# h of the second layer by one level of Strassen's algorithm over pairs of token blocks, with weights read back from DRAM

## The chip, the cores and the metric

The kernel runs on one core of one Trainium2 chip. The metric is the device time in microseconds of one execution; the number for the kernel before is the median of 3 runs. The trace comes from one further profiled execution of the same program.

## The reference

Attention through packed queries feeds two feed-forward layers. Only the second layer is touched by the change: x has 4608 rows (tokens) of 512, `w_in` is 512 x 2048, `w_out` is 2048 x 512.

```python
def _moe2_ref(x, w_in, w_out):
    h = x @ w_in
    g = h * np.cos(h)
    return (g @ w_out).astype(np.float32)
```

Everything is in float32. The kernel multiplies in a rounded 32-bit format (F32R) and wins accuracy back by splitting each operand into a high and a low part: a product is then three products, high x high, low x high and high x low.

## The kernel before, in words

The last half of the span is the second layer. Its tokens are cut into nine blocks of 512 (t = 0 to 8), its 2048 features into 16 blocks of 128, taken two at a time in eight steps (s = 0 to 7). In a step, `h2` makes h for two feature blocks: per feature block three part products (`wa, ya`) times four slices k of the contraction, so 24 matmuls of 128 x 512 a step. `el_cos` then computes g = h cos h on ScalarE (ACT) and VectorE (DVE) in turns: round (L586), fraction (L589), sine (L595), square (L596), product with h (L599), high part `gh` (L605), low part `gl` (L608). `ymm2` multiplies g by the rows of `w_out`, 24 matmuls a step, into four banks of PSUM that collect over the eight steps; after the last step they are copied out and stored. TensorE (PE) runs `h2` of step s+1 between `h2` and `ymm2` of step s, so that `el_cos` has the time of 24 other matmuls and more.

The weights of the second layer stay in SBUF as 32 tiles of the pool `wp` (16 `w2in`, 16 `w2out`, each with a high and a low part), and fill that pool. They are converted from 64-bit inputs by `Conv` in the last two blocks of the first layer and in block t = 0. The layer's input y1 lies in DRAM; `loady` and `splity` bring and split the next block's slices during a block, with the subtraction on GpSimd (POOL). The order on every engine is the order of the code (a manual schedule). All DMAs are issued by SyncE's queue (SP), in order: a DMA that waits holds up those behind it.

Of the kernel before, what the change touches and what calls it, by code (L numbers as in the profile page):

```python
# [10 lines left out]
F32 = mybir.dt.float32  # L11
F32R = mybir.dt.float32r
# [31 lines left out]
PACK1, PACK = 3, 7  # L44
G0, G1, G = (0, 14, 12), (7, 8, 22, 25), (9, 11, 13, 15)
YLOAD, Y2LOAD, Y2SPLIT = 2, 118, 125
SGN = -2147483648


@with_exitstack  # L50
def fused_kernel(ctx, tc, qT, kT, v, pT, w1i, w1o, w2i, w2o, ident, out):
# [17 lines left out]
    psh = ctx.enter_context(tc.tile_pool(name="psh", bufs=2, space=PSUM))  # L69
# [17 lines left out]
    class Conv:  # L87
# [525 lines left out]
    def ymm2(t, s, st):  # L613
        conv2.need(w2out, 2 * s + 1)
        if s == 0:
            yps[t] = [psy.tile([128, DM], F32, tag="y", name="y") for _ in range(4)]
        tail = (t, s) == (NB2 - 1, NSTEP - 1)
        for part, m in (
            [(i, m) for m in range(4) for i in range(2)] if tail
            else [(i, m) for i in range(2) for m in range(4)]  # L620
        ):
            for x in range(2):
                f = 2 * s + x
                for wh, gg in (((0, "gh"), (1, "gh")) if part == 0 else ((0, "gl"),)):
                    nc.tensor.matmul(  # L625
                        out=yps[t][m], lhsT=st[gg][:, x, 128 * m:128 * m + 128],
                        rhs=w2out[f][:, wh, :],
                        start=(s == 0 and x == 0 and part == 0 and wh == 0),
                        stop=(s == NSTEP - 1 and x == 1 and part == 1),
                    )  # L630
        if s == NSTEP - 1:
            for m in range(4):
                if m < 2:
                    o = p2.tile([128, DM], F32, tag="o", bufs=2, name="o")
                else:
                    o = p2r.tile([128, DM], F32, tag="wt", bufs=2, name="o")
                if m % 2 == 0:
                    nc.scalar.activation(out=o, in_=yps[t][m], func=AF.Copy, scale=-TWO_PI)
                else:
                    nc.vector.tensor_scalar(  # L640
                        out=o, in0=yps[t][m], scalar1=-TWO_PI, scalar2=None, op0=ALU.mult
                    )
                r0 = t * TB + 128 * m
                nc.sync.dma_start(out=out[r0:r0 + 128, :], in_=o)
            del yps[t]
# [147 lines left out]
    for n, (blk, s) in enumerate(steps):  # L793
        if n == NSTEP * (NB - 2):
            open_p2r()
            p2r, conv2 = p2x["r"], p2x["conv"]
        if n == STEP_ORDERED:
            sched.__exit__(None, None, None)
            sched = tc.manual_schedule()
            sched.__enter__()  # L800
        st = {}
        h1(blk, s, st)
        el1(st)
        cv = conv2 if blk >= NB - 2 else conv
        cv.c_all()
# [115 lines left out]
```

## Time and profile before

| | us |
|---|---|
| median of 3 runs (lowest, highest) | 1599.37 (1599.35, 1600.77) |
| the profiled execution, its own time | 1600.74 |
| its span, first to last instruction | 1599.0 |
| first matmul of h in the second layer starts at | 801.7 |
| last matmul of the second layer starts at, in the span | 1594.7 |
| busy over the span: PE, DVE, ACT, POOL | 1523.6, 1011.8, 871.4, 218.1 |

Read it as a chain: 1.7 us lie around the span, the first layer takes about half of it and the second layer the other half. An engine's busy time says little by itself; what counts is which engine the others wait for in a stretch.

### The profile page before, as it was taken

How to read it: one execution, taken by the hardware profiler on the slowest of the kernel's cores; microseconds unless marked ns; L12 is line 12 of the kernel's file. 1: busy time of each engine (PE TensorE's matmuls, PEld its weight loads, DVE VectorE, ACT ScalarE, POOL GpSimd, SP SyncE). 2: the span in 40 equal slices, each digit the busy share in tenths (PEclk: the TensorE clock that was granted, in tenths of full speed). 3: DMA queues.
4: the chain of work that ended last, by engine and by line, in shares of the span. 5: the costliest groups of instructions: out<-in, count | busy, mean ns of one | idle time of the engine just before them, and what ended most of it. 6: DMA issues, size and time to landing. Idle time of an engine off the chain costs nothing.

```text
span 1599.0 us, 25218 instructions
## 1 busy us (share of the span) xinstructions
PE 1523.6 (95%) x10336; PEld 1321.6 (83%) x10336; DVE 1011.8 (63%) x1357; ACT 871.4 (54%) x1331; POOL 218.1 (14%) x154
## 2 busy tenths in 40 slices
PE   3789999999999999997898999999999999999999
PEld 1678888999999999997877788888888888888887
DVE  6999888787878788789979433333333333333333
ACT  4768665665666566676666444444444443444443
POOL 3633110100101010111224010100001010101000
PEclk6799999999999999999999999999999999999999
DMA  9423222211211121022334101001010101010000
GB/s 347 147 100 119 78 79 90 64 46 34 76 36 58 60 64 60 31 80 95 94 114 139 40 14 40 14 1 53 0 47 7 42 12 40 14 40 14 23 4 27
DMA packets 49138, 97.63 MB, mean 61 GB/s; under 512 B 4928, under 2 KB 26432, under 8 KB 49024
## 3 DMA queue, kind: packets, MB, share of 16 engines
q1 hardware_dynamic: 49024, 96.03, 18.2%
q8 instruction: 81, 1.33, 0.4%
q14 instruction: 33, 0.27, 0.1%
HBM read 74.78 MB, written 21.23 MB: 60 GB/s over the span
## 4 chain that ended last, share of the span: by engine, by line
PE 78%; DVE 13%; issue 4%; ACT 2%; DMA 2%; SPq 0%; POOL 0%; DVEq 0%; ACTq 0%; POOLq 0%
PE y L625 22%; PE h L564 22%; PE y L500 20%; PE h L438 10%; DVE wt L133 2%; DVE y L468 2%; DVE wt L143 2%; PE gp L400 2%; DVE wt L138 2%; DVE d L466 1%; DVE t L465 1%; DVE y L472 1%; DVE gl L485 1%; ACT wt L121 1%; PE sc L250 1%
## 5 line engine op out<-in xcount | busy, mean ns | idle before, releaser
L564 PE MATMUL h<-yhl,w2i 128*128 128x512 f32 x1728 | 403.2, 389 | 0.0
L564 PEld LDWEIGHTS h<-yhl,w2i 128*128 128x128 f32 x1728 | 324.4, 188 | 67.1
L500 PE MATMUL y<-gh,w1o 128*128 128x288 f32 x2048 | 311.3, 304 | 16.8 <-ACT gh L480 11.8
L500 PEld LDWEIGHTS y<-gh,w1o 128*128 128x128 f32 x2048 | 284.1, 191 | 45.9 <-ACT t L453 14.9
L625 PE MATMUL y<-w2o,gh 128*128 128x512 f32 x1152 | 274.6, 390 | 7.4 <-ACT gh L605 7.4
L625 PEld LDWEIGHTS y<-w2o,gh 128*128 128x128 f32 x1152 | 215.7, 188 | 55.2 <-ACT gh L605 10.9
L589 DVE SCALAR_TENSOR_TENSOR a<-a,h 128x1024 f32<-128x1024 f32 (+1 forms) x74 | 88.0, 1192 | 244.9 <-ACT a L586 244.9
L438 PE MATMUL h<-a,g 128*128 128x288 f32 x1536 | 230.5, 300 | 12.8 <-ACT w1i L121 6.6
L438 PEld LDWEIGHTS h<-a,g 128*128 128x128 f32 x1536 | 214.9, 192 | 17.0 <-ACT w1i L121 7.5
L586 ACT ACTIVATE a<-h 128x1024 f32<-128x1024 f32 (+1 forms) x74 | 74.1, 1005 | 243.1 <-PE h L564 241.6
L453 ACT ACTIVATE t<-h 128x576 f32<-128x576 f32 x128 | 83.2, 650 | 207.6 <-PE h L438 207.3
L599 DVE SCALAR_TENSOR_TENSOR a<-a,h 128x1024 f32<-128x1024 f32 (+1 forms) x74 | 88.1, 1192 | 143.3 <-ACT a L596 143.3
L500 PE MATMUL y<-gl,w1o 128*128 128x288 f32 x1024 | 160.0, 299 | 1.2 <-DVE gl L485 1.2
L500 PEld LDWEIGHTS y<-gl,w1o 128*128 128x128 f32 x1024 | 145.0, 191 | 1.5 <-DVE gl L485 1.4
L625 PE MATMUL y<-w2o,gl 128*128 128x512 f32 x576 | 142.8, 390 | 0.0
L553 POOL TENSOR_TENSOR yhl<-yr,yhl 128x512 fp32r<-128x512 f32 x34 | 60.1, 1768 | 549.6 <-ACT yhl L552 549.6
L608 DVE TENSOR_TENSOR gl<-a,gh 128x1024 fp32r<-128x1024 f32 (+1 forms) x74 | 88.4, 1196 | 73.3 <-ACT gh L605 73.2
L465 DVE TENSOR_TENSOR t<-h,t 128x576 f32<-128x576 f32 x128 | 95.3, 744 | 52.8 <-ACT u L454 52.5
L625 PEld LDWEIGHTS y<-w2o,gl 128*128 128x128 f32 x576 | 108.2, 188 | 22.5 <-DVE gl L608 0.2
L472 DVE COPY_PREDICATED y<-k,t 128x576 f32<-128x576 int16 x128 | 118.4, 925 | 11.6
L595 ACT ACTIVATE a<-a 128x1024 f32<-128x1024 f32 (+1 forms) x74 | 76.7, 1037 | 83.3 <-DVE a L589 83.3
L605 ACT ACTIVATE gh<-a 128x1024 fp32r<-128x1024 f32 (+1 forms) x74 | 76.6, 1036 | 83.1 <-DVE a L599 83.1
(79 smaller groups left out, 1541.8 us busy)
## 6 DMA issues: line engine op xcount, KB each, us to landing
y<-ye SPq DMA_DIRECT2D x80, 144.0 KB, 1.9
yr<-y SPq DMA_DIRECT2D x36, 256.0 KB, 3.5
out<-o SPq DMA_DIRECT2D x36, 256.0 KB, 2.1
st<-w1i SPq DMA_DIRECT2D x16, 512.0 KB, 7.4
v<-vv SPq DMA_DIRECT2D x16, 512.0 KB, 4.5
st<-w1o SPq DMA_DIRECT2D x16, 512.0 KB, 6.5
st<-w2i SPq DMA_DIRECT2D x16, 512.0 KB, 3.6
st<-w2o SPq DMA_DIRECT2D x16, 512.0 KB, 3.6
```

The lines of the kernel that those rows point to most:

```text
L438: nc.tensor.matmul(out=h[:, x, 0:HB], lhsT=gw[b, f // 4, half][:, ga, c0:c0 + 128], rhs=a2[b, half][:, aa, HB * j:HB * j + HB], start=(n = ...
L453: nc.scalar.activation(out=st["t"], in_=h, func=AF.Tanh)
L465: lambda: nc.vector.tensor_tensor(out=t, in0=hs, in1=t, op=ALU.subtract),
L472: lambda: nc.vector.copy_predicated(out=y, mask=k.bitcast(I16), data=t),
L500: nc.tensor.matmul(out=yps[blk][d][:, 0:HB], lhsT=w1out[f][:, wh, 128 * d:128 * d + 128], rhs=st[gg][:, x, :], start=(s in first and x == ...
L564: nc.tensor.matmul(out=h[:, x, :], lhsT=w2in[f][:, wa, 128 * k:128 * k + 128], rhs=yt[k][:, ya, :], start=(n == 0), stop=(n == 11),)
L589: nc.vector.scalar_tensor_tensor(out=a[:, x], in0=a[:, x], scalar=MAGIC, in1=h[:, x], op0=ALU.subtract, op1=ALU.subtract,)
L595: nc.scalar.activation(out=a[:, x], in_=a[:, x], func=AF.Sin, scale=PI)
L599: nc.vector.scalar_tensor_tensor(out=a[:, x], in0=a[:, x], scalar=1.0, in1=h[:, x], op0=ALU.subtract, op1=ALU.mult,)
L605: nc.scalar.activation(out=gh[:, x], in_=a[:, x], func=AF.Copy)
L608: nc.vector.tensor_tensor(out=gl[:, x], in0=a[:, x], in1=f32(gh[:, x]), op=ALU.subtract)
L625: nc.tensor.matmul(out=yps[t][m], lhsT=st[gg][:, x, 128 * m:128 * m + 128], rhs=w2out[f][:, wh, :], start=(s == 0 and x == 0 and part == 0 ...
```

## The change: what it does

Blocks t = 0 to 2 are computed as before (`NCL` = 3). The other six are taken as three pairs (t, t+1). For a pair and a pair of feature blocks F, let A be the four 128 x 256 quarters of the transposed weights (two feature blocks by two halves of the contraction) and B the four quarters of the input (two halves of the contraction by two token blocks). Eight quarter products become seven (Winograd's form of Strassen's algorithm), of six matmuls each, with sums S1 to S4 of A and T1 to T4 of B as operands:

- P1 = A11 B11, P6 = S2 T2, P5 = S1 T1, P7 = S3 T3, P2 = A12 B21, P4 = A22 T4, P3 = S4 B22, in this order;
- DVE makes h of the two blocks from them by seven additions out of PSUM (`add`), into the SBUF tiles `ha` and `hb`.

The work of a pair has two phases. In phase A, for F = 0 to 7, PE makes the seven products (42 matmuls) and, between them, the 24 output matmuls of block t for F-1 or so, in three pieces (`chunks`, `pop`); ACT and DVE take ha through all of g and hb up to the product with h. In phase B, PE makes the 24 output matmuls a step of block t+1.

What has to be there for it: every converted weight tile is stored to DRAM (`wid`, `wod`, 32 tiles of 512 KB) by `store_w2`. During block t = 2 (steps 0 to 4) `combine` makes the weight sums S1 to S4 of each F on POOL, splits them on ACT and DVE and stores them (`wsd`). `bprep` makes B11, T1, T2, T3, B21, B22, T4, each high and low and for both slices j of the half, 40 operations for a pair: for the first pair in steps 5 to 7 of block t = 2, after that in phase B of the pair before. In phases A and B the weights are read back (`load_wa`, four DMAs for an F; `load_wo`, two for each F and block). The PSUM pool `psx` of four banks for the products takes the place of the two double banks of `h`.

```diff
+NCL, BPREP, COMBINE = 3, 5, ((0, 1), (2, 3), (4, 5), (6,), (7,), (), (), ())
...
+    def store_w2():
+        while stores:
+            kind, f, t = stores.pop(0)
+            nc.sync.dma_start(out=(wid if kind == "w2i" else wod)[f], in_=f32(t))
...
+    def combine(F):
...
+        nc.gpsimd.tensor_tensor(
+            out=w[:, 0, :], in0=f32(f0[:, 0, :]), in1=f32(f0[:, 1, :]), op=ALU.add
+        )
...
+            nc.gpsimd.tensor_tensor(out=c[:, i], in0=x, in1=y, op=op)
+        hi, lo = (p3.tile([128, 4, 256], F32R, tag="yhl", bufs=4, name="ws") for _ in range(2))
+        nc.scalar.activation(out=hi, in_=c, func=AF.Copy)
+        nc.vector.tensor_tensor(out=lo, in0=c, in1=f32(hi), op=ALU.subtract)
...
+    def bprep(t, bo):
...
+            ops += [
+                load, temp, s11[0], sub(t1, b12, b11), s11[1], s1[0], sub(t2, b22, t1), s1[1],
+                s2[0], sub(b12, b22, b12), s2[1], s21[0], s3[0], s21[1], sub(b21, b21, t2),
+                s3[1], s22[0], s4[0], s22[1], s4[1],
+            ]
...
+    def prod(wa, b):
+        dst = psx.tile([128, TB], F32, tag="p", name="p")
+        n = 0
+        for wi, bi in ((0, 0), (1, 0), (0, 1)):
+            for j in range(2):
+                nc.tensor.matmul(
+                    out=dst, lhsT=wa[wi][:, 128 * j:128 * j + 128], rhs=b[j][:, bi, :],
+                    start=(n == 0), stop=(n == 5),
+                )
+                n += 1
+        return dst
...
+                n = 1 if (t, s) == (NCL - 1, NSTEP - 1) else len(pend)
+                for fn in pend[:n]:
+                    fn()
+                pend = pend[n:]
...
+            if t == NCL - 1:
+                for F in COMBINE[s]:
+                    combine(F)
+                if s == BPREP:
+                    prep = bprep(NCL, bo)
+                if s >= BPREP:
+                    n = -(-len(prep) // (NSTEP - s))
+                    for fn in prep[:n]:
+                        fn()
...
+            P1 = prod(wa["A11"], bo["B11"])
+            P6 = prod(wa["S2"], bo["T2"])
+            P5 = prod(wa["S1"], bo["T1"])
...
+            nc.scalar.activation(out=p1, in_=P1, func=AF.Copy)
...
+            add(hb[:, 0], P6, p1)
...
+            pop()
+            P7 = prod(wa["S3"], bo["T3"])
+            P2 = prod(wa["A12"], bo["B21"])
+            add(hb[:, 1], P7, hb[:, 0])
+            add(ha[:, 0], P2, p1)
+            add(hb[:, 0], P5, hb[:, 0])
...
+            pop()
+            P4 = prod(wa["A22"], bo["T4"])
+            P3 = prod(wa["S4"], bo["B22"])
+            add(ha[:, 1], P4, hb[:, 1])
+            add(hb[:, 1], P5, hb[:, 1])
+            add(hb[:, 0], P3, hb[:, 0])
```

Where it moves instructions, first PE at the switch from block t = 2 to the first pair. Before, h of step (3, 0) follows, and then the output matmuls of (2, 7) (`Pool_49`, `DVE_49` and so on name the engine whose count a matmul waits for):

```order
L564 MATMUL h<-yhl,w2i 128x512 [waits PE_49]
L564 MATMUL h<-yhl,w2i 128x512 x7
L564 MATMUL h<-yhl,w2i 128x512 [waits Pool_49] x4
L564 MATMUL h<-yhl,w2i 128x512 x12
L625 MATMUL y<-w2o,gh 128x512 [waits Activation_49]
L625 MATMUL y<-w2o,gh 128x512 x15
L625 MATMUL y<-w2o,gl 128x512 [waits DVE_49]
L625 MATMUL y<-w2o,gl 128x512 x7
```

Now, from h of step (2, 7) on: 8 output matmuls of (2, 6), then P1 and most of P6 (L762).

```order
L577 MATMUL h<-yhl,w2i 128x512 x23
L634 MATMUL y<-w2o,gh 128x512 [waits Activation_49]
L634 MATMUL y<-w2o,gh 128x512 x7
L762 MATMUL p<-b,wa 128x512 [waits DMAHW4_49,DVE_49,PE_49]
L762 MATMUL p<-b,wa 128x512 [waits Activation_49]
L762 MATMUL p<-b,wa 128x512 x4
L762 MATMUL p<-b,wa 128x512 [waits DMAHW5_49]
L762 MATMUL p<-b,wa 128x512 [waits Activation_49]
L762 MATMUL p<-b,wa 128x512 [waits DMAHW6_49]
L762 MATMUL p<-b,wa 128x512 x2
L762 MATMUL p<-b,wa 128x512 [waits DVE_49]
```

What moved: the products of the pair stand directly behind 8 of the 24 output matmuls of (2, 6), the other 16 and those of (2, 7) behind the products. The DVE count for which the first matmul of P1 waits is that of L612 of step (2, 7), the last reader of the PSUM tile of h whose place P1 takes.

Second, DVE at the same place. Before, the three passes of steps (2, 6) and (2, 7) stand alone:

```order
L589 SCALAR_TENSOR_TENSOR a_11502<-a_11502,h_11477 128x1024
L599 SCALAR_TENSOR_TENSOR a_11502<-a_11502,h_11477 128x1024
L608 TENSOR_TENSOR gl_11504<-a_11502,gh_11503 128x1024
L589 SCALAR_TENSOR_TENSOR a_11561<-a_11561,h_11536 128x1024
L599 SCALAR_TENSOR_TENSOR a_11561<-a_11561,h_11536 128x1024
L608 TENSOR_TENSOR gl_11563<-a_11561,gh_11562 128x1024
```

Now (L602, L612 and L621 are the same three passes of step (2, 7); L723 is a low part, L730 a difference; `yq` the loaded input, `yt` T1 or T2):

```order
L723 TENSOR_TENSOR b_11729<-yq_11646,b_11729 128x512
L730 TENSOR_TENSOR yt_11737<-yq_11733 128x512
L723 TENSOR_TENSOR b_11738<-yq_11733,b_11738 128x512
L730 TENSOR_TENSOR yt_11737<-yq_11735,yt_11737 128x512
L602 SCALAR_TENSOR_TENSOR a_11770<-a_11770,h_11745 128x1024
L612 SCALAR_TENSOR_TENSOR a_11770<-a_11770,h_11745 128x1024
L621 TENSOR_TENSOR gl_11772<-a_11770,gh_11771 128x1024
L723 TENSOR_TENSOR b_11742<-yt_11737,b_11742 128x512
L730 TENSOR_TENSOR yq_11733<-yq_11735,yq_11733 128x512
L723 TENSOR_TENSOR b_11789<-yt_11737,b_11789 128x512
```

What moved: part of `bprep` for the second slice (j = 1) stands ahead of the passes of (2, 7) and waits for a load, and the low part of its T2, `b_11789`, which the last matmul of P6 reads, stands three operations behind them.

Third, PE in the middle of phase A, from P7 on, where `h2` and `ymm2` stood in turns of 24; no such rows are in the kernel before:

```order
L762 MATMUL p<-b,wa 128x512 [waits DVE_49]
L762 MATMUL p<-b,wa 128x512 x5
L762 MATMUL p<-b,wa 128x512 [waits Activation_49]
L762 MATMUL p<-b,wa 128x512 x5
L634 MATMUL y<-wo,gh 128x512 x8
L762 MATMUL p<-b,wa 128x512 [waits DMAHW7_49,DVE_49]
L762 MATMUL p<-b,wa 128x512 x5
L762 MATMUL p<-b,wa 128x512 [waits DVE_49]
L762 MATMUL p<-b,wa 128x512 x5
L634 MATMUL y<-wo,gl 128x512 x8
```

What moved: the 24 matmuls of an output step are cut into three pieces of 8 between the products (P7, P2, a piece, P4, P3, a piece). By its DVE count, P3 takes the bank of P7, freed by the addition that reads P7, and P5's bank goes to P5 of the next F.

## Rows read from the trace of the kernel before

**Rows 1.** Busy time of each engine in 100 us of the second layer (windows).

```profile
core 0: us, PE busy (x) PEld busy (x) DVE busy (x) ACT busy (x) POOL busy (x), PEclk, DMA share, GB/s
1100.00:1200.00 100.00, 100.00 (x443) 82.85 (x442) 35.17 (x31) 43.05 (x45) 9.41 (x6) 1.00 0.08 24
```

**Rows 2.** Timeline of one step there: start us, us, engine, line, operation [idle before].

```profile
1099.63 5.60 PE L564 MATMUL h<-yhl,w2i 128*128 128x512 f32 x24
...
1101.24 1.23 DVE L608 TENSOR_TENSOR gl<-a,gh 128x1024 fp32r<-128x1024 f32 x1 [1.12 <-ACT gh L605]
1101.80 1.83 POOL L553 TENSOR_TENSOR yhl<-yr,yhl 128x512 fp32r<-128x512 f32 x1 [52.57 <-ACT yhl L552]
...
1105.07 3.79 PE L625 MATMUL y<-w2o,gh 128*128 128x512 f32 x16
1105.27 1.03 ACT L586 ACTIVATE a<-h 128x1024 f32<-128x1024 f32 x1 [3.54 <-PE h L564]
1106.33 1.22 DVE L589 SCALAR_TENSOR_TENSOR a<-a,h 128x1024 f32<-128x1024 f32 x1 [3.87 <-ACT a L586]
1107.59 1.06 ACT L595 ACTIVATE a<-a 128x1024 f32<-128x1024 f32 x1 [1.29 <-DVE a L589]
...
1108.68 1.06 ACT L596 ACTIVATE a<-a 128x1024 f32<-128x1024 f32 x1
...
1109.77 1.22 DVE L599 SCALAR_TENSOR_TENSOR a<-a,h 128x1024 f32<-128x1024 f32 x1 [2.22 <-ACT a L596]
...
1110.51 5.60 PE L564 MATMUL h<-yhl,w2i 128*128 128x512 f32 x24
1111.03 1.06 ACT L605 ACTIVATE gh<-a 128x1024 fp32r<-128x1024 f32 x1 [1.29 <-DVE a L599]
...
1112.12 1.23 DVE L608 TENSOR_TENSOR gl<-a,gh 128x1024 fp32r<-128x1024 f32 x1 [1.13 <-ACT gh L605]
```

**Rows 3.** Groups by line: xcount, busy us, mean ns, idle before.

```profile
L564 PE MATMUL h<-yhl,w2i 128*128 128x512 f32 x1728 | 403.2, 389 | 0.0
...
L465 DVE TENSOR_TENSOR t<-h,t 128x576 f32<-128x576 f32 x128 | 95.3, 744 | 52.8 <-ACT u L454 52.5
...
L552 ACT ACTIVATE yhl<-yr 128x512 fp32r<-128x512 f32 x36 | 22.0, 616 | 0.0
```

**Rows 4.** The chain that ended last, its last 48 matmuls: start us, us.

```profile
1583.95 11.13 PE y L625 x48
```

**Rows 5.** DMA issues: xcount, KB each, median us from issue to landing.

```profile
yr<-y SPq DMA_DIRECT2D x36, 256.0 KB, 3.5
...
st<-w2i SPq DMA_DIRECT2D x16, 512.0 KB, 3.6
```

**Rows 6.** Windows with much DMA, columns as in group 1.

```profile
24.00:28.00 4.00, 0.58 (x16) 0.38 (x20) 4.00 (x9) 3.37 (x7) 2.60 (x2) 0.50 1.02 410
845.00:855.00 10.00, 8.59 (x39) 6.77 (x38) 9.57 (x10) 6.68 (x9) 4.90 (x4) 1.00 0.55 181
```

**Rows 7.** POOL's subtraction in the conversion: ns least/median/most.

```profile
L167 POOL TENSOR_TENSOR w2i<-wt,w2i x16: 1280/1302/1774, 712.7 to 882.0; 128x512 fp32r<-128x512 f32 x16
```

**Rows 8.** Granted clock in three windows, columns as in group 1.

```profile
58.00:60.00 2.00, 2.00 (x46) 1.54 (x45) 2.00 (x5) 2.00 (x6) 1.71 (x1) 0.73 0.00 0
...
789.00:791.20 2.20, 0.03 (x1) 0.03 (x1) 2.20 (x3) 0.76 (x2) 0.75 (x1) 1.00 0.93 364
...
1598.00:1599.00 1.00, 0.00 (x0) 0.00 (x0) 0.00 (x0) 0.00 (x0) 0.00 (x0) 0.74 0.00 0
```

**Rows 9.** PE's timeline around changes of clock and at a wait.

```profile
54.28 3.25 PE L438 MATMUL h<-a,g 128*128 128x288 f32 x12
...
62.36 1.83 PE L438 MATMUL h<-a,g 128*128 128x288 f32 x12
...
791.17 2.43 PE L500 MATMUL y<-gh,w1o 128*128 128x288 f32 x16 [3.04 <-ACT gh L480]
```

More of the change, by code (lines that the diff above doesn't have):

```diff
@@ L168, in c @@
             {"w1o": w1out, "w2i": w2in, "w2o": w2out}[kind][f] = t
+            if kind != "w1o":
+                stores.append((kind, f, t))
         def c_all(self):
@@ L611, in el_cos @@
         each("b")
[L613 to L629, printed above, removed]
-                    )
[L631 to L645, printed above, removed]
@@ new lines, in chunks, with part @@
+    def chunks(t, s, st):
+        def part(jobs):
+            if s == 0 and t not in yps:
+                yps[t] = [psy.tile([128, DM], F32, tag="y", name="y") for _ in range(4)]
+            for m, lo in jobs:
+                for x in range(2):
+                    w = st["wo"][x]
+                    for wh, gg in ((0, "gl"),) if lo else ((0, "gh"), (1, "gh")):
+                        nc.tensor.matmul(
+                            out=yps[t][m], lhsT=st[gg][:, x, 128 * m:128 * m + 128],
+                            rhs=w[:, wh, :],
+                            start=(s == 0 and x == 0 and not lo and wh == 0),
+                            stop=(s == NSTEP - 1 and x == 1 and lo),
+                        )
+                if s == NSTEP - 1 and lo:
+                    evac(t, m)
+        if s == NSTEP - 1:
+            groups = [[(m, False), (m, True)] for m in range(4)]
+        else:
+            groups = [
+                [(0, False), (1, False)], [(2, False), (3, False)], [(m, True) for m in range(4)]
+            ]
+        return [lambda g=g: part(g) for g in groups]
@@ new lines, in evac @@
+    def evac(t, m):
+        if m < 2:
+            o = p2.tile([128, DM], F32, tag="o", bufs=2, name="o")
+        else:
+            o = p2x["r"].tile([128, DM], F32, tag="wt", bufs=2, name="o")
+        if m % 2 == 0:
+            nc.scalar.activation(out=o, in_=yps[t][m], func=AF.Copy, scale=-TWO_PI)
+        else:
+            nc.vector.tensor_scalar(
+                out=o, in0=yps[t][m], scalar1=-TWO_PI, scalar2=None, op0=ALU.mult
+            )
+        r0 = t * TB + 128 * m
+        nc.sync.dma_start(out=out[r0:r0 + 128, :], in_=o)
@@ new lines, in prod, with add @@
+    def prod(wa, b):
+        dst = psx.tile([128, TB], F32, tag="p", name="p")
+        n = 0
+        for wi, bi in ((0, 0), (1, 0), (0, 1)):
+            for j in range(2):
+                nc.tensor.matmul(
+                    out=dst, lhsT=wa[wi][:, 128 * j:128 * j + 128], rhs=b[j][:, bi, :],
+                    start=(n == 0), stop=(n == 5),
+                )
+                n += 1
+        return dst
+    def add(out, x, y):
+        nc.vector.tensor_tensor(out=out, in0=x, in1=y, op=ALU.add)
@@ L849, in fused_kernel @@
     p2c, p2 = run_pool("p2")
-    hist = []
-    for t in range(NB2):
+    p3c, p3 = run_pool("p3")
+    pend, hist, bo = [], [], {}
+    for t in range(NCL):
         nyt = []
@@ new lines, in fused_kernel, with p4t, pop @@
+    hst["wo"] = [w2out[2 * hs + x] for x in range(2)]
+    pend += chunks(ht, hs, hst)
+    p3c.__exit__(None, None, None)
+    pshc.__exit__(None, None, None)
+    psxc = tc.tile_pool(name="psx", bufs=4, space=PSUM, reuse_waits="tile")
+    psx = psxc.__enter__()
+    p2x["c"].__exit__(None, None, None)
+    p2x["c"], p2x["r"] = run_pool("p4", side="right")
+    p4 = p2x["r"]
+    def p4t(tag, bufs=2):
+        return p4.tile([128, 2, TB], F32, tag=tag, bufs=bufs, name=tag)
+    def pop(n=1):
+        for _ in range(n):
+            if pend:
+                pend.pop(0)()
@@ new lines, in fused_kernel @@
+    pairs = list(range(NCL, NB2, 2))
+    wos = {}
+    for t in pairs:
+        A, Bs, lag = {}, [], []
+        for F in range(NSTEP):
+            wa = was.pop(0)
+            if F + 1 < NSTEP:
+                was.append(load_wa(F + 1))
+            wos[t, F] = load_wo(F)
+            if F == NSTEP - 1:
+                wob = [load_wo(0), load_wo(1)]
+            p1 = p4.tile([128, TB], F32, tag="p1", bufs=1, name="p1")
+            ea, eb = {"h": p4t("ha", 1)}, {"h": p4t("hb")}
+            ha, hb = ea["h"], eb["h"]
+            pa, pb = lag.pop(0) if lag else (None, None)
+            P1 = prod(wa["A11"], bo["B11"])
+            P6 = prod(wa["S2"], bo["T2"])
+            P5 = prod(wa["S1"], bo["T1"])
+            if pa:
+                e_sin(pa)
+            nc.scalar.activation(out=p1, in_=P1, func=AF.Copy)
+            if pa:
+                e_sq(pa)
+                e_sin(pb)
+            add(hb[:, 0], P6, p1)
+            if pa:
+                e_mul(pa)
+                e_gh(pa)
+                e_sq(pb)
+                e_gl(pa)
+            pop()
[4 more added lines that the diff above has]
+            add(hb[:, 0], P5, hb[:, 0])
+            if pb:
+                e_mul(pb)
+                pa["wo"] = wos.pop((t, F - 1))
+                pend.extend(chunks(t, F - 1, pa))
+            pop()
[4 more added lines that the diff above has]
+            add(hb[:, 0], P3, hb[:, 0])
+            ea["a"] = p2.tile([128, 2, TB], F32, tag="a", bufs=1, name="a")
+            if F % 2 == 0:
+                eb["a"] = a2p.tile([128, 2, S], F32, tag="a2", bufs=4, name="gt")[:, :, 0:TB]
+            else:
+                eb["a"] = wp.tile([128, 2, TB], F32, tag="w", name="gt")
+            e_round(ea)
+            e_frac(ea)
+            e_round(eb)
+            e_frac(eb)
+            lag.append((ea, eb))
+            Bs.append(eb)
+            pop()
+        last = t == pairs[-1]
+        for fn in (e_sin, e_sq, e_mul):
+            fn(ea)
+        e_sin(eb)
+        e_gh(ea)
+        e_sq(eb)
+        e_gl(ea)
+        e_mul(eb)
+        pop(3)
+        ea["wo"] = wos.pop((t, NSTEP - 1))
+        pend.extend(chunks(t, NSTEP - 1, ea))
+        if not last:
+            bo = {}
+            prep = bprep(t + 2, bo)
+            was = [load_wa(0)]
+        else:
+            prep = []
+        for F in range(NSTEP):
+            if F + 2 < NSTEP:
+                wob.append(load_wo(F + 2))
+            e_gh(Bs[F])
+            e_gl(Bs[F])
+            n = -(-len(prep) // max(1, 6 - F))
+            for fn in prep[:n]:
+                fn()
+            prep = prep[n:]
+            Bs[F]["wo"] = wob.pop(0)
+            pend.extend(chunks(t + 1, F, Bs[F]))
+            keep = 6 if not last and F == NSTEP - 1 else (3 if F < NSTEP - 1 else 0)
+            pop(len(pend) - keep)
```

113 lines of the change are left out of this document (105 added, 8 removed).

## The prediction, made before the result was known

> **What bounds the kernel now.** I read the windows first. In 100 us of the second layer PE is busy for all 100, DVE for 35, ACT for 43, POOL for 9, and the DMA engines move 24 GB/s [rows 1]: PE sets the pace there and everything else has room. The timeline gives that pace. h of one step starts at 1099.63, of the next at 1110.51 [rows 2]: 10.88 us for 48 matmuls, 0.2267 us each, of which the 24 of h take 5.44. The same rows give the latency behind a step: h is complete when the output matmuls start at 1105.07; from there `gh` is ready after 7.02 us (1111.03 + 1.06) and `gl` after 8.28, the product with h (L599) after 5.92. `gh` is wanted after 10.88. So 3.9 us of delay on ACT or DVE cost nothing, and what a matmul saves is worth its 0.2267 us as long as PE stays fed.
>
> **What is removed.** h takes 1728 matmuls over nine blocks [rows 3], 192 a block. For a pair and an F, 48 become 42; three pairs by eight F make 144 fewer: 144 x 0.2267 = 32.6 us. Output matmuls stay. The cut last step goes too: the chain's last 48 matmuls took 11.13 us [rows 4] against 10.88; in the new tail all of g is ready long before, so 0.25 us are gained.
>
> **What phase A adds.** PE takes 66 matmuls an F, 14.96 us. DVE does seven additions out of PSUM and five passes of 1024. An addition of a PSUM and an SBUF operand took 744 ns for 576 columns [rows 3], so about 0.66 for 512, 0.69 with the gap to the next; a pass 1.22 [rows 2]: together 10.9 of 14.96 us. ACT does seven passes of 1.06 and a copy of 0.62 [rows 2, 3], 8.0 us. Then the waits, counted from the start of P1: P3 starts at 11.8 and wants the bank that the addition of P7 frees (P7 ends at 7.3; free at 8.2). P4 starts at 10.4, its bank is free at 3.6; P2 at 7.2, its bank after the copy, 2.2. P1 of the next F wants P2's bank (9.6 against 15.0), P6 that of P4 (12.7 against 16.3), P5 that of P5 (13.4 against 17.7). All have 3 us or more. I take nothing for phase A.
>
> **What phase B adds.** 24 matmuls, 5.44 us a step; DVE needs `gl` and four operations of `bprep` (1.22 + 4 x 0.72 = 4.1), ACT about 3. PE enters it after P3 of F = 7 with four pieces left (7.25 us); by the chain of passes `gh` of the last F takes 6.8. Margin 0.4 us: nothing, bound 1.5 for each of three pairs.
>
> **What the loads add.** An F of phase A reads 1.8 MB of `wa` and 1 MB of `wo`, 187 GB/s over 14.96 us; phase B with `wo`, the next input, `wa` and the outputs about 300. The queue has moved 410 GB/s at a share of 1.02 [rows 6]. In SP's order the tiles of F+1 wait for nothing later than the products of F-1, so they land about one F ahead. Nothing; the bound is a rival below. The stores of block t = 0 share a stretch that DVE bounds (9.57 of 10 us) at 181 GB/s [rows 6]; at most twice that is still below 410, and a conversion's load of 3.6 us [rows 5] is issued two tiles ahead of the one that ACT reads. Nothing, bound 3.
>
> **The weight sums in t = 2.** For an F, POOL does two operations of 512 and four of 256. One of 512 took 1.30 (median) [rows 7], and 1.83 when DVE's `gl` ran beside it [rows 2]; halved for 256, an F costs 5.2 to 7.3 us, two F a step 10.4 to 14.6 against a step of 10.88. POOL starts ahead, in t = 1, by two F, and then falls up to 3.8 us behind each step for three steps. ACT's copy of a sum stands in front of the next step's round. At the slow price the round of step 3 comes 3.8 to 4.0 us late, against the 3.9 of slack: 0.2 us. I take that, bounds 0 and 5. The Trainium skill's page SBUF — State Buffer (Who interferes with whom) states that a DVE instruction with two SBUF inputs and a GpSimd instruction that reads SBUF exclude each other for a whole instruction. The 1.83 against 1.30 agree with it. By it POOL loses up to three passes a step (`gl` and two low parts, 3.7 us), 14.1 us a step, by the free price none; the slow price above is nearly the same.
>
> **The switch to the first pair** is where I expect the loss. Count from the end of h of (2, 5). DVE's `gl` ends at 8.3; seven operations of `bprep` (0.69 each, 0.72 with the gap) follow, ACT's third difference comes at 12.6, so the round of (2, 6) starts 1.5 late and its `gl` ends at 20.7. The next difference, at 21.4, frees the tile into which j = 1 is loaded; a load takes 3.5 us [rows 5]: 25.0. Difference, 25.7; its high part on ACT, 26.4; only then ACT rounds (2, 7), whose h was ready at 21.76: 4.4 late. PE meanwhile does its 8 output matmuls until 23.6 and meets P1, which takes the place of h of (2, 7) and waits for L612: 21.76 + 5.92 + 4.4 = 32.1. That is a wait of 8.6 us. P6 then waits for the low part of T2, three operations behind `gl` of (2, 7): 33.2 + 1.2 + 3 x 0.72 = 36.6, where it could have ended at 34.9: 1.9 more. Behind that, the 16 left output matmuls cover the rest. Sum 10.5 us; lower bound 5.5 (loads and queue not late), upper 14.
>
> A wait of 3.04 us left the granted clock at 1.00 [rows 8, 9]; in the 3.9 us behind the last matmul it fell (0.74 on the average of the last one), so 8.6 us take it to the lower level of 1.2 GHz. From dense matmuls at 54.28 it took until the window 58 to 60 (0.73 on the average) to come back, and 12 matmuls took 3.25 us there, 1.83 later [rows 8, 9]: a factor of 1.78. Some 4.8 us at that level lose 2.1, about half of it inside P6's wait. I take 1.0, bounds 0 and 2.5. That PE's clock is gated by its own activity and falls after idling is also what the Trainium skill says (TensorE: Matmul & The Clock Gate, Part 1); by a wait without it the sum would be 1.0 less.
>
> **The sum.** 1600.74 - 32.64 - 0.25 + 10.5 + 1.0 + 0.2 = 1579.55 against the profiled execution; the median of the runs is 1.37 below that execution: **1578.2 us**, 1.3% faster.
>
> **The rivals.**
> 1. *Slower: loads one at a time.* An F of phase A has five loads of 512 KB and one of 256: if each landed before the next moved, 5 x 3.6 + 3.5 = 21.5 us against 14.96, 6.5 us an F, 24 times: 1734 us. What is left of the gain, 21 us, is gone from 0.9 us an F on. Against it: 410 GB/s on the same queue is nearly three times the single rate of 146 [rows 5, 6]. Chance 0.06.
> 2. *Slower: a bank held too long.* P5 is read twice, the second time after P4. If a product behind P4 had to wait for P5's bank, PE would idle for two additions and the end of the matmul, 1.6 us, each F: 24 x 1.6 = 38, 1617 us. By the order P3 takes P7's bank; this needs additions that are much slower from PSUM than rows 3. Chance 0.05.
> 3. *The weight sums hold ACT.* With POOL slower still (256 columns cost nearly what 512 do, 11 us an F), steps 1 to 4 of t = 2 stall by some 8 us: 1586. The exclusion on the page named above works this way. Chance 0.09.
> 4. *No gap at the switch.* If the passes of (2, 7) run on time, P6's operand is 4.4 earlier and the clock stays: 1573, or 1567 with no wait at all. Chance 0.07.
> 5. *No change*: rivals 2 or 3 in part, some 20 us in all. Chance 0.03.
>
> **How the numbers follow.** My forecast has 0.70. Its own range adds the bounds: down by 5 (gap), 1.0 (clock) and 0.2 to 1572, up by 3.5 (gap), 1.5 (clock), 5 (sums) and part of 3 (stores) and 4.5 (ends of phase A) to 1591. Rival 4's nearer value and rival 3 are inside or beside it; the range is 1571 to 1592. 0.2% is about what a measurement of this kernel can tell from no change. Faster 0.86, the same 0.03, slower 0.11.
>
> **What would show it.** 1584 matmuls of h and products in place of 1728; 0.2267 us a matmul in phases A and B, PE busy 100% there; no wait of PE on P3 or P4; DVE near 73% in phase A; `wa` landing an F ahead; one PE wait of 8 to 9 us ended by L612 at the first P1, a second of some 2 us ended by L723, then a few us at half clock; ACT's L683 waiting for POOL by step 3 of t = 2. PE waiting on loads in each F, or on an addition in each F, would make the prediction wrong.

## The result, and the profile after

Median 1577.9 us (1577.37 to 1579.48) against 1599.36 before (1599.14 to 1600.77): ratio 0.9866, interval 0.9849 to 0.9883. The forecast was 1578.2. The profiled execution took 1577.37 us, its span 1575.5. A change of 1% in a whole says little about its terms, so below I use a stretch that leaves the first layer out: from the first `h` matmul of the second layer to the start of the last two output matmuls, called **layer 2**. It was 801.69 to 1594.46 before, 792.77 us, and is 800.39 to 1571.29 now, 770.90 us: 21.87 us less. The first layer was 1.3 us shorter in this execution, though it runs the same matmuls; it varies by about 3 us among the executions below.

First, three windows of the changed kernel that answer to [rows 1]: phase A of the first pair (to 1191) and a little of its phase B; the end of that phase A with most of its phase B; phase A of the second pair.

```profile
1100.00:1200.00 100.00, 100.00 (x442) 82.64 (x441) 72.14 (x82) 54.00 (x57) 0.00 (x0) 1.00 0.61 219
1180.00:1230.00 50.00, 50.00 (x222) 41.24 (x221) 35.50 (x45) 25.43 (x32) 0.00 (x0) 1.00 0.73 273
1250.00:1350.00 100.00, 100.00 (x443) 82.81 (x442) 72.73 (x84) 53.56 (x58) 0.00 (x0) 1.00 0.68 242
```

PE still has no gap and its full clock, and it does 442 or 443 matmuls in 100 us, as before (443): the pitch, the time from the start of one matmul to that of the next, is the same 0.2267 us. DVE went from 35 to 72, ACT from 43 to 54, DMA from 24 to 219 GB/s, and none of them is waited for. Next, all waits of PE between 780 and 1580.

```profile
PE y L634 <- ACT gh L618: 8.2, 8, 1.4
PE p L762 <- DVE a L612: 7.6, 1, 7.6
PE y L513 <- ACT gh L493: 4.4, 3, 3.1
```

The third row belongs to the first layer. Of the first, 7.5 us in 7 waits belong to block 0 (7.4 before), and one wait of 0.69 to block 2, where the kernel before has none. So the change brought two waits: 7.6 us at the switch to the first pair, and this one:

```profile
1016.89 3.79 PE L634 MATMUL y<-w2o,gh 128*128 128x512 f32 x16
...
1020.48 1.06 ACT L683 ACTIVATE ws<-cs 128x1024 fp32r<-128x1024 f32 x1 [5.00 <-POOL cs L681]
...
1021.44 1.01 ACT L599 ACTIVATE a<-h 128x1024 f32<-128x1024 f32 x1
...
1028.62 3.92 PE L634 MATMUL y<-w2o,gh 128*128 128x512 f32 x16 [0.69 <-ACT gh L618]
```

`h` of (2, 3) was complete at 1016.89, but ACT rounded it (L599) only at 1021.44, behind its copy of a weight sum (L683), which waited 5.00 us for POOL. That is 4.55 late, 0.65 more than the 3.9 that cost nothing. The groups of the page:

```profile
L762 PE MATMUL p<-b,wa 128*128 128x512 f32 x1008 | 242.2, 391 | 7.6 <-DVE a L612 7.6
...
L577 PE MATMUL h<-yhl,w2i 128*128 128x512 f32 x576 | 134.3, 389 | 0.0
```

1008 + 576 = 1584 matmuls where there were 1728 [rows 3]. Now the switch itself, from the timeline of the changed kernel (start us, us, engine, line, operation; in brackets the wait before it and what ended it):

```profile
1060.20 0.93 SPq L736 DMA_DIRECT2D yq<-y  x2
...
1061.39 1.97 PE L634 MATMUL y<-w2o,gh 128*128 128x512 f32 x8
...
1063.86 0.63 ACT L720 ACTIVATE b<-yq 128x512 fp32r<-128x512 f32 x1 [3.05 <-DMA yq<-y]
...
1065.19 1.01 ACT L599 ACTIVATE a<-h 128x1024 f32<-128x1024 f32 x1
...
1069.66 1.22 DVE L612 SCALAR_TENSOR_TENSOR a<-a,h 128x1024 f32<-128x1024 f32 x1 [2.21 <-ACT a L609]
...
1070.98 6.23 PE L762 MATMUL p<-b,wa 128*128 128x512 f32 x18 [7.62 <-DVE a L612]
...
1074.35 0.69 DVE L723 TENSOR_TENSOR b<-yt,b 128x512 fp32r<-128x512 f32 x1
...
1077.05 1.98 PE L634 MATMUL y<-w2o,gh 128*128 128x512 f32 x8
```

`h` of (2, 7) was complete at 1061.39, but ACT rounded it only at 1065.19: it stood behind an operation of `bprep` that waited 3.05 us for the load of j = 1. PE had 8 output matmuls, then waited until L612 had read that `h`. Behind the wait, P1, P6 and P5 took 6.07 us (1070.98 to 1077.05), where 18 x 0.2267 = 4.08. The windows say why (columns as in [rows 1], the granted clock before the last two):

```profile
1066.00:1069.00 3.00, 0.00 (x0) 0.00 (x0) 1.22 (x1) 1.68 (x3) 0.00 (x0) 0.85 1.02 373
1069.00:1071.00 2.00, 0.02 (x1) 0.05 (x1) 1.22 (x1) 0.71 (x2) 0.00 (x0) 0.50 1.07 405
1071.00:1073.00 2.00, 2.00 (x5) 1.61 (x6) 1.00 (x1) 2.00 (x3) 0.00 (x0) 0.50 0.99 322
1073.00:1075.00 2.00, 2.00 (x7) 1.52 (x6) 2.00 (x5) 0.55 (x2) 0.00 (x0) 0.51 1.05 410
1075.00:1077.00 2.00, 2.00 (x10) 1.65 (x9) 1.97 (x5) 1.22 (x4) 0.00 (x0) 1.00 0.86 352
```

The clock fell in the wait to its lower level and came back at about 1075: 5 and 7 matmuls in 2 us, then 10. So the switch cost 7.6 us of wait and 2.0 of clock. From start to start it is 9.77 us, because the view counts a wait from the modelled end of a matmul (0.39 us long), 0.16 behind the place of the next one.

### The profile page after: what moved, and what is told of

Its sections match the earlier page's. It is cut to its first block, busy times and chain, and to the rows that moved or that the text cites. A ratio compares the mean times of both kernels' runs of the same rounds, so it can differ in the third digit from the quotient of the medians.

```text
span 1575.5 us, 25882 instructions
## 1 busy us (share of the span) xinstructions
PE 1491.6 (95%) x10192; PEld 1293.6 (82%) x10192; DVE 1170.5 (74%) x1596; ACT 897.3 (57%) x1377; POOL 227.2 (14%) x178
## 4 chain that ended last, share of the span: by engine, by line
PE 74%; DVE 15%; issue 4%; ACT 4%; POOL 2%; DMA 1%; SPq 0%; DVEq 0%; POOLq 0%; ACTq 0%
PE y L634 21%; PE y L513 20%; PE p L762 15%; PE h L451 10%; PE h L577 4%; DVE wt L144 2%; PE gp L413 2%; DVE wt L154 2%; DVE wt L149 2%; DVE y L481 1%; DVE t L478 1%; DVE d L479 1%; POOL cs L681 1%; PE pp L320 1%; DVE y L485 1%
## 5 line engine op out<-in xcount | busy, mean ns | idle before, releaser
L762 PE MATMUL p<-b,wa 128*128 128x512 f32 x1008 | 242.2, 391 | 7.6 <-DVE a L612 7.6
L451 PE MATMUL h<-a,g 128*128 128x288 f32 x1536 | 229.7, 299 | 14.6 <-ACT w1i L132 7.1
L762 PEld LDWEIGHTS p<-b,wa 128*128 128x128 f32 x1008 | 190.5, 189 | 47.8 <-issue 8.0
L634 PE MATMUL y<-wo,gh 128*128 128x512 f32 x768 | 188.1, 389 | 0.0
L634 PEld LDWEIGHTS y<-wo,gh 128*128 128x128 f32 x768 | 144.1, 188 | 30.0
L577 PE MATMUL h<-yhl,w2i 128*128 128x512 f32 x576 | 134.3, 389 | 0.0
L577 PEld LDWEIGHTS h<-yhl,w2i 128*128 128x128 f32 x576 | 108.1, 188 | 22.4
L498 DVE TENSOR_TENSOR gl<-y,gh 128x576 fp32r<-128x576 f32 x128 | 102.8, 803 | 6.8 <-ACT gh L493 6.6
L634 PE MATMUL y<-w2o,gh 128*128 128x512 f32 x384 | 93.8, 392 | 8.2 <-ACT gh L618 8.2
L481 DVE SCALAR_TENSOR_TENSOR y<-y,d 128x576 f32<-128x576 f32 x128 | 101.4, 792 | 0.1
L634 PE MATMUL y<-wo,gl 128*128 128x512 f32 x384 | 97.8, 389 | 0.0
```

Source lines behind the costliest of these rows:

```text
L451: nc.tensor.matmul(out=h[:, x, 0:HB], lhsT=gw[b, f // 4, half][:, ga, c0:c0 + 128], rhs=a2[b, half][:, aa, HB * j:HB * j + HB], start=(n = ...
L481: lambda: nc.vector.scalar_tensor_tensor(out=y, in0=y, scalar=PC0 - PC1 * PC1 / (4 * PC2), in1=d, op0=ALU.add, op1=ALU.mult,),
L498: nc.vector.tensor_tensor(out=st["gl"], in0=st["g"], in1=f32(st["gh"]), op=ALU.subtract)
L577: nc.tensor.matmul(out=h[:, x, :], lhsT=w2in[f][:, wa, 128 * k:128 * k + 128], rhs=yt[k][:, ya, :], start=(n == 0), stop=(n == 11),)
L634: nc.tensor.matmul(out=yps[t][m], lhsT=st[gg][:, x, 128 * m:128 * m + 128], rhs=w[:, wh, :], start=(s == 0 and x == 0 and not lo and wh == 0),
L762: nc.tensor.matmul(out=dst, lhsT=wa[wi][:, 128 * j:128 * j + 128], rhs=b[j][:, bi, :], start=(n == 0), stop=(n == 5),)
```

## The experiments

The theory: the matmuls are worth their pitch, phases A and B run free, and nearly the whole loss is one gap, which comes from ACT and DVE being late with the chain of (2, 7). Rivals: loads, banks, weight sums. Ratios are against the kernel before on the same chip; changes of layer 2 are against the 770.90 of the changed kernel, from one profile each (a second profile of the changed kernel, under e13, has 770.99).

**e1_fill.** All output matmuls of (2, 6) ahead of the first product.

```diff
-                n = 1 if (t, s) == (NCL - 1, NSTEP - 1) else len(pend)
+                n = len(pend)
```

> All three pieces of the output matmuls of (2, 6) run before the first product, not one. Theory: the wait at the first product is set by when L612 of (2, 7) ends, not by PE, so the 16 more matmuls (3.6 us) fit into it and the wait falls from 7.6 to about 4.0; the second loss there, 2.0 us of matmuls at half clock, turns in part into a wait of P6 for its operand, which is ready at a fixed time: together 4.0 us are gained at the switch. But the queue of pieces is then two pieces shorter all through the first phase A, and at its end PE has 3.6 us of work where gh of the last F needs 6.8: about 3.2 us are given back there, about 1576.9 us in all. Rival: the pieces are only filler, and nothing is given back: 1573.9.

1579.29 us, ratio 0.9863 (0.9848 to 0.9877); layer 2 772.69, 1.8 longer. The first wait fell by as much as the 16 matmuls fill, from 7.6 to 3.9, and another came at the end of the first phase A. PE's timeline:

```profile
1070.40 6.05 PE L762 MATMUL p<-b,wa 128*128 128x512 f32 x18 [3.88 <-DVE a L612]
...
1190.07 1.98 PE L634 MATMUL y<-wo,gl 128*128 128x512 f32 x8
1194.87 2.08 PE L634 MATMUL y<-wo,gh 128*128 128x512 f32 x4 [2.82 <-ACT gh L794]
```

That return is what the theory says; that the sum got worse is not. The windows of the same kernel at the second wait:

```profile
1192.00:1194.00 2.00, 0.04 (x1) 0.00 (x0) 1.23 (x1) 1.65 (x3) 0.00 (x0) 1.00 0.00 0
1194.00:1196.00 2.00, 1.13 (x3) 0.94 (x4) 1.15 (x2) 2.00 (x3) 0.00 (x0) 0.53 0.00 0
1196.00:1198.00 2.00, 2.00 (x6) 1.54 (x5) 2.00 (x3) 1.23 (x2) 0.00 (x0) 0.50 0.00 0
```

The clock fell behind it too: the 16 matmuls from 1194.87 to 1201.45 took 6.58 us in place of 3.63, 2.95 more. With 1.8 at the switch (18 matmuls in 6.05 us, to the modelled end of the last, where the changed kernel had 6.23), two waits of 3.9 and 2.8 cost 11.5 us, one of 7.6 had cost 9.6: the 1.8 to 1.9 more that were measured.

**e2_fill_hold.** The same, and two of the pieces kept back in the first step of the pair, so that the end of phase A has its cover again.

```diff
-            pop()
+            if (t, F) != (NCL, 0):
+                pop()
...
```

> As the run before, but F = 0 of the first pair holds its first two pieces back, so that the queue is as long as in the changed kernel afterwards. Theory: the gain at the switch stays, nothing is given back at the end of phase A: about 1573.9 us, PE's wait at the first product about 4.0 us and none behind L794 at the end of the first phase A. Products back to back in F = 0 should not wait for banks. Rival: the wait at the first product grows back because ACT or DVE, not the order on PE, sets the start of all of F = 0: 1577 to 1578.

1574.95 us, ratio 0.9833 (0.9819 to 0.9848); layer 2 767.08, 3.8 shorter. One wait of 4.0 us is left at the first product, none at the end of phase A. A filler helps when it comes from where it isn't needed.

**e3_no_wa.** Weights are loaded for F = 0 alone and used for every F, which changes `h` of the pairs; loads of W_out stay.

```diff
-            wa = was.pop(0)
-            if F + 1 < NSTEP:
-                was.append(load_wa(F + 1))
+            wa = was[0]
+            was = [wa]
+            was.append(wa)
```

> The loads of wa for F = 1 to 7 are left out (the weights of F = 0 are used for all F, so h is computed with wrong weights): 1.8 MB of 2.8 MB an F less on the queue in phase A. Theory: the loads land about one F ahead and cost nothing: within 1 us of the changed kernel, 1577 to 1579. Rival: read-back or its traffic costs PE something in each F, then it is faster, by 5 us or more if each F lost 0.2 us.

1578.08 us, ratio 0.9856 (0.9842 to 0.9871); layer 2 770.73. From 1100 to 1200 DMA moved 127 GB/s instead of 219 and PE was at 100.00 in both. The loads of these weights cost nothing in the pairs, and nothing there waited for those of W_out: rival 1 falls.

**e4_ncl5.** Five blocks in the old way and two pairs (`NCL` = 5).

```diff
-NCL, BPREP, COMBINE = 3, 5, ((0, 1), (2, 3), (4, 5), (6,), (7,), (), (), ())
+NCL, BPREP, COMBINE = 5, 5, ((0, 1), (2, 3), (4, 5), (6,), (7,), (), (), ())
```

> Blocks t = 0 to 4 as before, two pairs in place of three. Theory: a pair saves 48 matmuls of 0.2267 us = 10.9 us and the switch costs the same 9.6 us however many pairs follow: 1577.9 + 10.9 = 1588.8 us. Rival: a pair has hidden costs of its own (ends of phases, loads), then less than 10.9 is lost, down to some 6 us.

1589.74 us, ratio 0.9925 (0.9908 to 0.9941); layer 2 781.75, 10.85 longer. A pair is worth 48 x 0.2267 = 10.88, to 0.03 us: a pair has no cost of its own, and the gap (7.8 us of wait here) and the wait behind the weight sums (0.66, now in block 4) are paid once.

**e7_prep_fill** and **e8_prep.** The loads for the first pair early and both at once, in buffers of the weight pool, its operations spread over more steps, the weight sums a step shorter; e7 on e2, e8 on the changed kernel.

```diff
-NCL, BPREP, COMBINE = 3, 5, ((0, 1), (2, 3), (4, 5), (6,), (7,), (), (), ())
+NCL, COMBINE = 3, ((0, 1), (2, 3), (4, 5), (6, 7), (), (), (), ())
+PREP = (0, 0, 0, 0, 15, 13, 3, 9)
...
+                    if t == NCL:
+                        q[n, j] = wp.tile([128, 2, TB], F32, tag="w", name="yq")
...
```

> e2_fill_hold with the first pair's inputs made earlier: its four loads are issued together in step 4 of block 2 into buffers of the weight pool, their 40 operations are spread as 15, 13, 3 and 9 over steps 4 to 7, and the eight sums of weights end in step 3. Theory (the gap at the switch is the lateness of the last chain, which stands behind operations that wait for the loads of the second half): sine chain of step (2,7) about 4 us earlier, the first product's wait 4.0 -> 0 to 0.5 us, and the slow clock behind it (some 2 us in e2_fill_hold) gone with it: 5 to 6 us under e2_fill_hold, ratio near 0.980. Rival (the chain itself is what is late, or the loads only wait elsewhere): wait near 4 us again, ratio 0.983.

> The same earlier inputs in the changed kernel itself, whose last step still keeps two of three groups of output products for later, so that only 8 output products (1.8 us) cover the last chain. Theory: the first product's wait 7.6 -> about 3.8 us, since the chain ends 3.6 to 4 us earlier; the clock still falls behind that wait; 3.5 to 4.5 us under the changed kernel, ratio near 0.984. Rival (lateness from elsewhere): 7.6 us again, 0.9866.

e7: 1575.41 us, ratio 0.9844 (0.983 to 0.9859), layer 2 767.49. e8: 1581.29 us, ratio 0.9883 (0.9868 to 0.9898), layer 2 773.14. The gap did shrink, in e7 to 1.35 us at full clock, in e8 to 5.0. But e7 gained nothing on e2, and e8 lost 2.2 us of layer 2 on the changed kernel: both expectations missed. The timeline of e7 in block 2:

```profile
1027.90 1.05 ACT L684 ACTIVATE ws<-cs 128x1024 fp32r<-128x1024 f32 x1
...
1028.05 3.93 PE L635 MATMUL y<-w2o,gh 128*128 128x512 f32 x16 [0.66 <-ACT gh L619]
...
1033.91 1.06 ACT L684 ACTIVATE ws<-cs 128x1024 fp32r<-128x1024 f32 x1 [4.96 <-POOL cs L682]
1034.88 1.01 ACT L600 ACTIVATE a<-h 128x1024 f32<-128x1024 f32 x1
...
1041.95 3.94 PE L635 MATMUL y<-w2o,gh 128*128 128x512 f32 x16 [2.72 <-ACT gh L619]
```

ACT waits 4.96 us for POOL's sums in front of the round (L600) of the next step, whose `gh` is then 2.7 late for PE. The 0.66 is the wait that the changed kernel has too; the 2.72, and 0.44 and 0.54 later, are new. From start to start e7 pays 4.6 us more than e2 in block 2 for 4.3 less at the switch. The 2.72 is my rival 3, brought about by two sums in step 3. The two smaller waits have a second cause: in those steps operations of the first pair stand in front of the round on ACT as well (five of them from 1042.59 on, the round only at 1046.73). In e8 the same wait of 2.71 also cost the clock (16 matmuls 5.52 us, in e7 3.94): 4.6 us more in block 2 for 2.4 less at the switch.

**e9_bank_first** (on e7) and **e10_bank_after** (on the changed kernel). The products' banks as a plain ring of four that begins with the banks free since (2, 6); in the changed kernel the first product's bank is one that `h` of (2, 7) holds.

```diff
-        dst = psx.tile([128, TB], F32, tag="p", name="p")
+        psx.append(psx.pop(0))
+        dst = psx[-1].tile([128, TB], F32, tag="p", name="p")
...
+    psx = psx[2:] + psx[:2]
...
```

> e7_prep_fill with the products' four banks in another order: the first two products go to the banks that have been free since step (2,6), where so far the first product is put into a bank that step (2,7)'s h still holds. Theory: with the chain on time the bank waits for nobody, so the same time as e7_prep_fill within 1 us; if a wait for the chain's last pass is left there, this takes it away and the difference is that wait. Rival (order of banks costs something in the pairs): slower by a wait in every step, seen in the waits of the products.

> The changed kernel with only the order of the banks changed, as in e9_bank_first. Theory of two limits close together: P1 no longer waits (7.6 -> 0), but P6 then waits for the low part of T2, which DVE makes behind the same late chain (ready at 1075.0 in the profile of the changed kernel, where P6 and P5 ended at 1077.1): the gap goes to P6, and the gain is 0.4 us or less, or nothing if the longer pause costs more of the clock. Rival (the bank alone sets the gap): 7.6 us less, ratio 0.982.

e9: 1618.48 us, ratio 1.0116 (1.0101 to 1.0131), layer 2 810.41, 42.9 more than e7. e10: 1622.63 us, ratio 1.0141 (1.0124 to 1.0158), layer 2 815.44. I had expected e9 level with e7; its rival came true. For e10 I had not thought of waits in the pairs at all. PE's largest wait in e9, and a step of it:

```profile
PE p L769 <- DVE hb L777: 36.3, 24, 1.6
```

```profile
1099.67 1.65 PE L769 MATMUL p<-b,wa 128*128 128x512 f32 x6 [1.51 <-DVE hb L777]
```

In a plain ring P3, the fourth product behind P5, gets P5's bank, which DVE reads last (`hb` + P5, behind `ha` + P4). That is the mechanism of rival 2 of the prediction: I had put it at 1.6 us a step; it is 42.9 / 24 = 1.79 a step, the 1.51 of the view, the 0.16 named above, and 0.13 that the six matmuls behind the wait take longer (1.65 us; 1.52 where nothing waits). The pool of the changed kernel hands out banks in the order 4, 7, 6, 5, 4, 7, 5, so that P3 follows P7. The clock stayed at 1.00 through all 24 waits.

The switch of e10 answers the other question, what else stands close behind the bank:

```profile
1069.56 2.24 PE L763 MATMUL p<-b,wa 128*128 128x512 f32 x7 [3.64 <-DMA wa<-wid]
...
1074.82 2.07 PE L763 MATMUL p<-b,wa 128*128 128x512 f32 x4 [3.03 <-ACT b L720]
...
1077.37 2.93 PE L763 MATMUL p<-b,wa 128*128 128x512 f32 x6 [0.47 <-DVE b L723]
```

P1 no longer waits for the bank, but its weights land at 1069.5: SP issued them behind the two late loads of `yq`. Then P6 waits for the high and the low part of T2. Together 7.1 us in place of 7.6, and with the clock at its lower level from about 1071 to 1081 the switch costs 10.7 us from start to start, where it had cost 9.8: three limits lie side by side, all behind the late loads and the late chain. The weights as a limit I had not seen.

**e11_spread** and **e12_spread_bank.** Both on e2: weight sums as in the change, only the loads a step earlier, operations in the order of need. e12 also gives P1 the bank that is free since (2, 6), and P5 the one that `h` of (2, 7) holds; as in the changed kernel P5 is alone in its bank (P2, P4 and P3 after P1, P6 and P7).

```diff
+PREP = (0, 0, 0, 0, 2, 15, 7, 16)
...
+            a = [1, 2, 3, 4, 5, 6, 7, 8, 10]
+            b = [0, 9, 12, 15, 11, 13, 14, 17, 19, 16, 18]
+            both = [i + k for i in b for k in (0, 20)]
+            ops = [ops[i] for i in both[:2] + a + [i + 20 for i in a] + both[2:]]
...
```

> e2_fill_hold with the sums of weights where the change has them (steps 0 to 4), the first pair's four input loads issued together in step 4 into buffers of the weight pool, and its operations put in the order in which the products want them (T2 and T1 first), 15 in step 5, 7 in step 6, 16 in step 7. Theory (e7_prep_fill shortened the gap at the switch to 1.35 us at full clock and lost it again in block 2, where two sums of weights in step 3 kept the sine chains behind GpSimd): no waits for gh in block 2 beyond those of block 0 (8.2 us), a wait of 0.5 to 1.4 us at the first product, full clock there; layer 2 some 4 to 5 us shorter than in e2_fill_hold, ratio near 0.981. Rival (the waits of block 2 come from the input operations themselves): waits for gh of 2 to 4 us again and 0.984.

> e11_spread with each product given a fixed bank: P1 and P6 the two that have been free since step (2,6), P5 and P7 those of step (2,7)'s h; P2, P4 and P3 reuse those of P1, P6 and P7, and no product follows P5 in its bank within a step. Theory (in e9_bank_first and e10_bank_after a plain ring of four put P3 into P5's bank, which is read last, 1.5 us in each of 24 steps): no wait of the products on DVE's sums, and the wait that e11_spread has left at the first product gone: 0 to 1.4 us less than e11_spread, within 0.1% of it. Rival (any fixed order costs waits in the pairs): 24 waits again, tens of us.

e11: 1574.47 us, ratio 0.9842 (0.9827 to 0.9857), layer 2 767.58. e12: 1576.24 us, ratio 0.9853 (0.9836 to 0.9869), layer 2 768.25. Block 2 has no wait beyond the changed kernel's (0.6) and the pairs none for banks, as the theories said; but no time was gained on e2, where 4 to 5 us were expected. e12:

```profile
1068.74 6.29 PE L771 MATMUL p<-b,wa 128*128 128x512 f32 x24
...
1076.33 2.27 ACT L721 ACTIVATE b<-yq 128x512 fp32r<-128x512 f32 x4 [3.26 <-DVE yq L731]
...
1078.51 0.58 ACT L1088 ACTIVATE p<-p 128x512 f32<-128x512 f32 x1
1079.13 6.63 PE L771 MATMUL p<-b,wa 128*128 128x512 f32 x18 [4.10 <-ACT p L1088]
```

Four products run without a long wait from 1068.74 on; then P2 waits 4.1 us for ACT's copy of P1, which stands behind the last 16 input operations, and the clock falls (18 matmuls take 6.48 us to 1085.61, not 4.08). e11 has the same in two parts, 2.1 us at the first product and 2.4 for the copy.

**e13_prep_late** and **after_again.** e12 with the last eight input operations behind that copy and two more behind the last chain; and the changed kernel on the same chip.

```diff
-PREP = (0, 0, 0, 0, 2, 15, 7, 16)
+PREP = (0, 0, 0, 0, 2, 15, 5, 10)
...
             add(hb[:, 0], P6, p1)
+            while prep:
+                prep.pop(0)()
...
```

> e12_spread_bank with the last eight input operations (for P4 and P3) moved behind ACT's copy of P1 and the first sum of the first step of pair 0, and two of the operations ahead of the last chain moved behind it. Theory (e12_spread_bank's first four products ran without a wait, and its 4.1 us came later, at P2, since ACT's copy of P1 stood behind 16 input operations): copy of P1 about 4 us earlier, a wait of 0 to 1.2 us in all over the first step, full clock in it, layer 2 about 5 us shorter than in e12_spread_bank (768.2 us) and ratio near 0.982. Rival (ACT and DVE have too much to do in that stretch, whatever the order): again 3 to 4 us of wait, now at P4, and 0.985.

> The changed kernel once more, unedited, on the same chip as e13_prep_late, for a direct comparison: ratio 0.985 to 0.988, first product's wait 7.6 us; layer 2 about 771 us.

e13: 1571.01 us (1570.27 to 1572.78), ratio 0.9815 (0.9801 to 0.9828). The changed kernel: 1576.95 (1576.49 to 1580.22), 0.9855 (0.9841 to 0.9868). e13 beats both kernels, the changed one by 5.9 us; layer 2 763.51 against 770.99. Its timeline:

```profile
1067.77 6.96 PE L771 MATMUL p<-b,wa 128*128 128x512 f32 x30
...
1071.36 0.57 ACT L1088 ACTIVATE p<-p 128x512 f32<-128x512 f32 x1
...
1075.23 1.66 PE L771 MATMUL p<-b,wa 128*128 128x512 f32 x6 [0.50 <-ACT b L721]
...
1078.29 1.62 PE L771 MATMUL p<-b,wa 128*128 128x512 f32 x6 [1.40 <-DVE hb L779]
```

30 matmuls without a stop, the copy 7 us earlier than in e12, 1.9 us of wait left (P4 for T4, P3 for the bank of P7, whose sum is behind four low parts on DVE), and the granted clock at 1.00 from 1064 to 1082. e13 differs from e12 in the order of these operations alone, and that gave 4.7 us of layer 2, 5 expected. Which of the earlier edits e13 still needs, no run tried.

## Why the prediction was right, step by step

- **Removed matmuls, 32.64, and the last step, 0.25.** Right: 144 fewer at their pitch, and e4 measures a third of it as 10.85 against 10.88. From the start of the last 48 matmuls to that of the last two it is 10.43 us, before 10.67.
- **Phases A and B: nothing.** Right: no wait, DVE at 72.1 and 72.7% in the windows of 100 us above (I worked out 73), ACT at 54 (53.5). The margin of 0.4 us at the end of phase A held; e1 shows it to be small, since taking 16 matmuls (3.6 us) away from there brought a wait of 2.8. By that it is some 0.7, an estimate.
- **Loads: nothing.** Right, by the waits of PE and, for `wa`, by e3. On the page `wo` lands 6.5 us after its issue and `wa` 5.5 to 6.2, within an F.
- **Gap, 10.5.** The step that was mis-sized. The first half was right in place and cause, 7.6 for 8.6: the round of (2, 7) was 3.8 late (1065.19 against 1061.39), I had 4.4. The second, 1.9 for P6's wait on the low part of T2, did not appear: that part was ready at 1075.04, and P6, at the lower clock, was not stopped by it.
- **Clock, 1.0.** Too small: 2.0, and it hid the wait just named. At the full pitch P6's last matmul would have stood at 1073.47, 1.6 us before that part. So the two terms can't be added as I did; together gap and clock are 9.77 from start to start against 11.5.
- **Weight sums, 0.2.** Right in place and mechanism, too small: 0.69 of wait, and 0.98 from start to start (that step took 11.86 us in place of 10.88). Two F took POOL 14.0 us (1006.47 to 1020.44; I had 14.1 to 14.6); the round of step 3 came 4.55 late and not 4.0. An operation of 256 columns took 0.74, not half of 1.30; beside DVE's two-input passes up to 1.72. The Trainium skill (SBUF — State Buffer, Who interferes with whom) says that such a pair of instructions excludes each other; the 0.74 and 1.72 agree. e7 shows what one sum more in a step costs, a wait of 2.72. No run took the 0.69 away; e13 has it still (0.6).
- **Stores in block 0: nothing.** Right within 0.2 us: from its first `h` matmul to the first of its last output step block 0 took 96.82 us, before 96.66.

By these terms layer 2 should be 32.64 + 0.24 - 9.77 - 0.98 - 0.16 = 21.97 us shorter; it is 21.87. Against the forecast of the profiled execution (1579.55) 2.2 us are missing: 1.7 from the switch, 1.3 from the first layer, 0.2 behind the last matmul, less 0.8 for the weight sums and 0.2 for block 0. That forecast and median lie only 0.3 us apart is luck: the first layer's 1.3 was in no term, and I took the median to be 1.37 below the profiled execution, where it is 0.53 above.

Of the rivals, 1 is refuted by e3, 2 by the changed kernel's own waits, 5 by the interval, and 3 came true in small, 0.98 us of its 8. e9 and e7 made 2 and 3 real by a small edit and found 2's price near, 1.79 for 1.6 a step; that e9's 1618 lies by the 1617 is chance, since e9 starts from e7. 4 is what e13 comes to: 1571.0, between its 1573 and 1567. What the gap comes from was harder to settle than I thought when I took the chain alone: e10 and e12 show that curing one limit only uncovers the next (bank, weights, T2, copy of P1), and that these wait for one queue of operations on ACT and DVE, the weights for the late loads ahead of them on SP. Only when the copy of P1, too, had its place by need (e13) did the time go.

## What to carry to other kernels

Where PE is the bound and its neighbours have slack, price a saved matmul by its pitch and look for the loss where the schedule changes form, not in the steady state; there list every operand that the first matmul and its followers need, since several are late together, and order the feeding engines by need. Price a wait of PE with the clock behind it: two shorter waits can cost more than a long one. And which bank follows which is part of the algorithm: a product whose bank is read last wants a successor that comes late.

## What the runs showed of the hardware that I had not expected

Short waits can cost the clock, and not always. A wait of 3.04 us before [rows 8, 9] and one of 2.72 in e7 left it at full speed; waits of 2.71 (e8) and 2.82 (e1) were followed by a stretch at half speed that lost 1.7 and 2.95 us, and 24 waits of 1.5 us with some 15 us of matmuls between them never moved it. In e11 one of 2.1 left it and one of 2.4 took it down. The Trainium skill (TensorE: Matmul & The Clock Gate, Part 1) says that the gate follows PE's recent activity and that the moment at which it opens varies from run to run; two nearly equal waits with different ends (2.72 and 2.71) show a variation of that kind where it falls.
